# Casting transfers for the high parts of weights, and a shorter warm-up of TensorE

## The chip, the cores and the metric

The kernel runs on one core of a Trainium2 chip. The metric is the device time of one execution in microseconds (us). PE is TensorE, DVE is VectorE, ACT is ScalarE, POOL is GpSimd, SP is SyncE, which only issues transfers here.

## The reference

A causal convolution with seven taps per head, softmaxed over the taps, is followed by two blocks of two matrix products with an activation in between.

```python
w = softmax(weight, axis=-1)                            # 8 heads, 7 taps
x = causal_conv(x, w)                                   # 2 x 4096 tokens of 192 channels: 8192 x 192
h = x @ moe_w_in                                        # 192 -> 2048
g = np.where(h >= 1, h, np.where(h <= -1, 0.0, (h + 1) ** 2 / 4))
x = g @ moe_w_out                                       # 2048 -> 192
h = x @ moe2_w_in
out = (h / (1.0 + np.exp(-1.702 * h))) @ moe2_w_out
```

The weights arrive as 64-bit floats, everything else as 32-bit floats.

## The kernel before

The 8192 tokens are cut into 16 blocks of 512. Channels lie on partitions: part a is channels 0 to 127, part b the other 64, two blocks of part b in one tile. A phase is one block through one of the two matrix blocks `n` (1 or 2); it has 16 units, one for each 128 hidden channels (index `f`). A unit is five products into a bank `h` (`gemm1`), the activation (`act_a`), a split of its result into `ghi` and `glo` (`act_b`), and five products into the accumulators `acc` (`gemm2`), four units later (`LAG`).

To keep fp32 precision with the fast fp32r format, each operand is split into a high part, the value rounded to fp32r, and a low part, the rest: `split` casts on ACT (L74) and subtracts on DVE (L75). Products of high and low parts are added up in the same bank.

A weight tile is 128 x 448 words for each `n` and `f`, 32 tiles in all. It is loaded once as raw 64-bit words (`raw`) and turned into fp32 by integer operations, then split. `weight_ops` gives four pieces: `begin` (L118 on ACT, L119 on DVE), `join` (L123 on DVE), `high_part` (L129, a cast on ACT, or on DVE for the six tiles of `BY_DVE`) and `low_part` (L133 and L134 on DVE). The result lies in `wt` for the whole run. The first four tiles (`f < CH`, `n == 1`) are converted in the opening. The others follow a plan by steps: a step is one unit on TensorE, and `convert_at` puts the four pieces of a tile on four steps in a row, behind the unit's own work. Every engine takes its instructions in the order in which they are written (the schedule is manual).

In the opening TensorE first runs a warm-up, products of the identity with itself. The convolution of the first blocks is split between DVE (part a of block 0, tile `cva`), and TensorE with ACT and POOL: for each tap, a diagonal matrix (`diag`, the identity times the tap, L170) is multiplied with the shifted tile `xt`, seven products into `cb_ps` for part b of blocks 0 and 1 (diagonals made by ACT) and seven into `ca_ps` for part a of block 1 (diagonals made by POOL). `put_a` and `put_b` split the results into `xah`, `xal` and `xb`. These products are plain fp32, which the profile lists as two rows each. The opening's order on DVE and ACT is written out by hand:

```python
order = a0[0:5] + ws[0][0:1]
order += [lambda: nc.scalar.activation(table, ident[:, 0:1], AF.Gelu_apprx_sigmoid)]
order += ws[0][1:3] + a0[5:7] + ws[0][3:4] + ws[1][0:1] + [lambda: put_a(0, ca)]
order += ws[1][1:2] + [lambda: put_b(0, cb_ps)] + ws[1][2:] + ws[2]
```

Here `a0` are the seven convolution steps of block 0 on DVE, `ws[f]` the four pieces of weight tile `f`. The first unit's products need `wt`, `xah`, `xal` and, for the fourth and fifth, `xb`.

Of the kernel before, what the change touches and what calls it, by code (L numbers as in the profile page):

```python
# [8 lines left out]
F32 = mybir.dt.float32  # L9
F32R = mybir.dt.float32r  # L10
U32 = mybir.dt.uint32
# [4 lines left out]
P = 128  # L16
T = 512
# [3 lines left out]
def kernel(  # L21
# [21 lines left out]
    nc = tc.nc  # L43
    NBLK, D, _ = out.shape
    K = taps_in.shape[2]
    NF, _, WC = w1.shape
# [4 lines left out]
    LAG = 4  # L51
    CH = 4
    WHOLE = 2 * NF
    BY_DVE = {(1, f) for f in range(CH, NF, 3)} | {(2, 0), (2, 3)}

    const = ctx.enter_context(tc.tile_pool(name="const", bufs=1))
    wpool = ctx.enter_context(tc.tile_pool(name="wpool", bufs=1))
    stage = ctx.enter_context(tc.tile_pool(name="stage", bufs=2))
# [2 lines left out]
    xs_p = ctx.enter_context(tc.tile_pool(name="xs", bufs=4))  # L61
    a_p = ctx.enter_context(tc.tile_pool(name="a", bufs=3))
    g_p = ctx.enter_context(tc.tile_pool(name="g", bufs=LAG))
    o_p = ctx.enter_context(tc.tile_pool(name="o", bufs=2))
    ps = ctx.enter_context(tc.tile_pool(name="ps", bufs=1, space=bass.MemoryType.PSUM))

    def bank(n, name):
        return ps.tile([P, T], F32, tag=f"bank{n}", name=name)

    def f32(ap):  # L70
        return ap.bitcast(F32)
# [6 lines left out]
    taps = const.tile([P, 2, K], F32, name="taps")  # L78
    ident = const.tile([P, P], F32, name="ident")
    const.tile([P, 56], F32, name="pad")  # L80

    def softmax_taps():
        mx = const.tile([P, 2], F32, name="mx")
        sm = const.tile([P, 2], F32, name="sm")
        nc.vector.tensor_reduce(mx, taps, axis=AX.X, op=ALU.max)
        nc.vector.tensor_sub(taps, taps, mx.unsqueeze(2).to_broadcast([P, 2, K]))
        nc.scalar.activation(taps, taps, AF.Exp)
        nc.vector.tensor_reduce(sm, taps, axis=AX.X, op=ALU.add)
        nc.vector.tensor_scalar_add(sm, sm, 1e-9)
        nc.vector.reciprocal(sm, sm)  # L90
        nc.vector.tensor_mul(taps, taps, sm.unsqueeze(2).to_broadcast([P, 2, K]))


    words = {1: w1, 2: w2}
    wt = {n: wpool.tile([P, NF, 2 * WC], F32R, name=f"wt{n}") for n in (1, 2)}

    def weight_load(n, f):
# [4 lines left out]
    def weight_ops(n, f, s):  # L102

        low, high = s[:, :, 0], s[:, :, 1]  # L110
        w = wt[n][:, f, :]
        m = WC - DB
        st = {}

        def begin():
            a = stage.tile([P, WC], F32, tag="wa", name="wa")
            d = stage.tile([P, WC], U32, tag="wd", name="wd", bufs=3)
            nc.scalar.activation(a, f32(high), AF.Prelu, scale=2.0**-112, alpha=-(2.0**32))  # L118
            nc.vector.tensor_single_scalar(d, low, 29, op=ALU.logical_shift_right)  # L119
            st["a"], st["d"] = a, d  # L120

        def join():
            nc.vector.scalar_tensor_tensor(  # L123
                st["d"], st["a"].bitcast(U32), 3, st["d"], op0=ALU.logical_shift_left, op1=ALU.bitwise_or
            )

        def high_part():
            cast = nc.vector.tensor_copy if (n, f) in BY_DVE else nc.scalar.copy
            cast(w[:, 0:WC], f32(st["d"]))  # L129

        def low_part():
            d = f32(st["d"])
            nc.vector.tensor_sub(w[:, WC + DB : 2 * WC], d[:, 0:m], f32(w[:, 0:m]))  # L133
            nc.vector.tensor_sub(w[:, WC : WC + DB], d[:, m:WC], f32(w[:, m:WC]))  # L134

        return [begin, join, high_part, low_part]


    x1, x2 = {}, {}

    def new_xs():
        return [xs_p.tile([P, T], F32R, tag=t, name=t) for t in ("xah", "xal", "xb", "xc")]
# [16 lines left out]
    def warm_up():  # L159

        w = bank(7, "warm")
        wide = ident.unsqueeze(1).to_broadcast([P, T // P, P])
        for _ in range(4):
            nc.tensor.matmul(w.rearrange("p (k c) -> p k c", c=P), ident, wide, start=True, stop=True)  # L164

    def conv_on_pe(part, t, c, ident, eng_mul):

        d = o_p.tile([P, K, P], F32, tag="o", name="diag")
        for k in range(K):
            eng_mul(d[:, k], ident, taps[:, part, k : k + 1])  # L170

        def tap(k):
            return lambda: nc.tensor.matmul(c, d[:, k], t[:, k : k + T], start=k == 0, stop=k == K - 1)  # L173

        return [tap(k) for k in range(K)]

    def put_a(i, c):
        split(c, *x1[i][:2])
# [236 lines left out]
    plan, xt, raw = {}, {}, {}  # L415

    def at(step, op):
        plan.setdefault(max(step, 0), []).append(op)

    def fetch_w(n, f):  # L420
        raw[n, f] = weight_load(n, f)

    def weights_at(n, f):
        ops = []

        def piece():
            if (n, f) in raw:
                ops.extend(weight_ops(n, f, raw.pop((n, f))))
            ops.pop(0)()

        return [piece] * 4

    def fetch_x(*which):
        for part, i in which:
            xt[part, i] = x_load(part, i)
# [11 lines left out]
    with tc.manual_schedule():  # L447
        nc.sync.dma_start(taps, taps_in)
        fetch_x((0, 0), (1, 0))
        fetch_w(1, 0)  # L450
        fetch_w(1, 1)
        fetch_x((0, 1))
        fetch_w(1, 2)

        make_identity(nc, ident)
        warm_up()
        softmax_taps()

        table = const.tile([P, 1], F32, name="table")
        for i in range(B):  # L460
            x1[i] = new_xs()
        ca = cv_p.tile([P, T], F32, tag="cva", name="cva")
        cb_ps, ca_ps = bank(3, "cb_ps"), bank(2, "ca_ps")
        a0 = conv_taps(0, xt[0, 0], ca)
        b_ops = conv_on_pe(1, xt[1, 0], cb_ps, ident, nc.scalar.mul)
        a1 = conv_on_pe(0, xt[0, 1], ca_ps, ident, nc.gpsimd.tensor_scalar_mul)
        for op in b_ops + a1[:1]:
            op()

        ws = [weight_ops(1, f, raw.pop((1, f))) for f in range(CH - 1)]  # L470
# [4 lines that stand above are left out]
        for op in order:  # L475
            op()
        fetch_w(1, 3)
        for k, op in enumerate(weights_at(1, 3)):
            at(k // 2, op)
        for k, op in enumerate(a1[1:]):  # L480
            at(1 + k // 3, op)
        at(1, lambda: put_b(1, cb_ps))
        at(2, lambda: put_a(1, ca_ps))

        def convert_at(n, f, steps):
            at(steps[0] - 3, lambda: fetch_w(n, f))
            for step, op in zip(steps, weights_at(n, f)):
                at(step, op)

        for f in range(CH, NF):  # L490
            s = f - 2 if f < 2 * CH else 2 * CH - 1 + 5 * (f - 2 * CH) // 3
            convert_at(1, f, range(s, s + 4))
        for f in range(NF):
            s = (22, 23, 25, 26, 28, 29, 30, 31)[f] if f < NF // 2 else 36 + (3 * f - 3 * NF // 2) // 2
            convert_at(2, f, range(s, s + 4))
        for j in range(1, NBLK // B):
            conv_at(j)

        def beside(step):
            for op in plan.get(step, []):  # L500
                op()

        def finish_if_last(u, step):
            if 0 <= u < len(units) and units[u][1] == NF - 1:
                finish(units[u][0], step)


        for step in range(WHOLE):
            gemm1(step)
            if step >= LAG:  # L510
                gemm2(step - LAG)
            act_a(step)
            finish_if_last(step - LAG, step)
            if step >= 1:
                act_b(step - 1)
            if step == WHOLE - 1:
                act_b(step)
            beside(step)

        for u in range(WHOLE, len(units) + LAG + 4, 2):  # L520
            v = u - LAG
            if u == WHOLE:
                gemm1(u)
                gemm2(v)
                gemm1(u + 1)
                gemm2(v + 1)
            elif u < len(units):
                both(u, v)
            elif v < len(units):
                gemm2(v)  # L530
                gemm2(v + 1)
            if u < len(units):
                for op in (act_a, act_b):
                    op(u)
                    op(u + 1)
            for step in (u, u + 1):
                beside(step)
            finish_if_last(v + 1, u + 1)
# [55 lines left out]
```

## Time and profile before

| | |
|---|---|
| median of 3 runs | 1132.95 us (1132.06 to 1133.93) |
| profiled execution | 1132.19 us, its span 1130.4 us |
| PE busy | 1125.0 us, 9458 matmuls |
| weight loads (PEld) | 948.5 us |
| DVE busy | 716.0 us |
| ACT busy | 820.2 us |
| POOL busy | 6.5 us, 13 instructions |
| granted TensorE clock | 1.000 over the span |

The span runs from the first to the last instruction; the time of the execution holds about 1.8 us more. Times in the trace are counted from the start of the span. Ends of matmuls are modelled, so their starts say more than their lengths. The granted clock is listed as full for the whole span, the opening included.

### The profile page before, as it was taken

What the parts mean: (1) busy time and instruction counts of PE and PEld (TensorE: products, weight loads), DVE (VectorE), ACT (ScalarE), POOL (GpSimd) and SP (SyncE); (2) the same over time, 40 slices, a digit from 0 to 9 for tenths busy, and PEclk for the clock granted to TensorE, in tenths of its full rate; (3) what the DMA queues carried; (4) which work ended last, traced back from release to release, by engine and by line L of the source; (5) the groups of instructions that cost most, each with busy time, mean ns of one, the idle gap of its engine ahead of it and who ended that gap; (6) DMA issues with size and microseconds to landing.
All of it is one profiled execution on the core that took longest, in us unless ns stands there. A gap on an engine that the chain in (4) does not pass through costs nothing.

```text
span 1130.4 us, 23108 instructions
## 1 busy us (share of the span) xinstructions
PE 1125.0 (100%) x9458; PEld 948.5 (84%) x9458; DVE 716.0 (63%) x1158; ACT 820.2 (73%) x1462; POOL 6.5 (1%) x13
## 2 busy tenths in 40 slices
PE   9999999999999999999999999999999999999998
PEld 5888888888888888888888888888888888888887
DVE  7998867775647656475664756657566575655532
ACT  7998768867768677676876758677586776868654
POOL 2000000000000000000000000000000000000000
PEclk9999999999999999999999999999999999999999
DMA  5434111000010000100010000100001000000000
GB/s 160 135 112 159 34 34 44 11 20 15 11 39 15 20 15 14 36 15 20 15 41 22 1 20 15 48 15 1 20 15 48 15 1 20 15 20 15 11 15 15
DMA packets 16840, 36.68 MB, mean 32 GB/s; under 512 B 2528, under 2 KB 2784, under 8 KB 16736
## 3 DMA queue, kind: packets, MB, share of 16 engines
q1 hardware_dynamic: 16592, 35.09, 10.8%
q8 instruction: 74, 1.21, 0.5%
q14 instruction: 30, 0.25, 0.1%
q10 hardware_dynamic: 144, 0.13, 0.0%
HBM read 21.05 MB, written 6.29 MB: 24 GB/s over the span
## 4 chain that ended last, share of the span: by engine, by line
PE 100%; issue 0%; POOL 0%; ACT 0%; POOLq 0%
PE acc L366 48%; PE h L366 43%; PE acc L320 3%; PE h L255 3%; PE cb_ps L173 1%; PE ca_ps L173 1%; PE warm L164 0%; ACT o L410 0%; POOL ident masks.py:199 0%; POOL ident masks.py:197 0%; POOLq masks.py:199 0%; ACT o L408 0%; POOLq L580 0%
## 5 line engine op out<-in xcount | busy, mean ns | idle before, releaser
L366 PE MATMUL acc<-ghi,wt 64*128 64x512 f32 x2868 | 871.0, 386 | 0.0
L366 PE MATMUL h<-xah,wt 64*128 64x512 f32 x1912 | 738.2, 386 | 0.0
L366 PE MATMUL acc<-glo,wt 64*128 64x512 f32 x1912 | 706.7, 386 | 0.0
L366 PEld LDWEIGHTS acc<-ghi,wt 64*128 64x128 f32 x2868 | 490.9, 184 | 47.8
L75 DVE TENSOR_TENSOR glo<-a,ghi 128x512 fp32r<-128x512 f32 x512 | 341.6, 688 | 231.2 <-ACT ghi L74 220.9
L366 PEld LDWEIGHTS h<-xah,wt 64*128 64x128 f32 x1912 | 351.8, 184 | 32.4 <-issue 0.4
L366 PEld LDWEIGHTS acc<-glo,wt 64*128 64x128 f32 x1912 | 351.8, 184 | 32.2 <-DVE glo L75 0.2
L366 PE MATMUL h<-xal,wt 64*128 64x512 f32 x956 | 369.1, 386 | 0.0
L74 ACT CAST ghi<-a 128x512 fp32r<-128x512 f32 x512 | 301.5, 614 | 28.6 <-DVE a L279 28.4
L279 DVE SCALAR_TENSOR_TENSOR a<-h,a 128x512 f32<-128x512 f32 x256 | 176.8, 691 | 157.1 <-ACT a L278 156.7
L281 ACT ACTIVATE a<-h 128x512 f32<-128x512 f32 x256 | 150.3, 595 | 147.8 <-PE h L366 136.6
L366 PE MATMUL h<-xc,wt 64*128 64x512 f32 x717 | 238.7, 386 | 0.0
L366 PE MATMUL h<-xb,wt 64*128 64x512 f32 x717 | 238.7, 386 | 0.0
L277 ACT ACTIVATE a<-h 128x512 f32<-128x512 f32 x256 | 151.0, 590 | 53.9 <-PE h L366 53.3
L366 PEld LDWEIGHTS h<-xal,wt 64*128 64x128 f32 x956 | 175.9, 184 | 16.0
L278 ACT ACTIVATE a<-a 128x512 f32<-128x512 f32 x256 | 161.9, 632 | 8.2
L366 PEld LDWEIGHTS h<-xc,wt 64*128 64x128 f32 x717 | 131.9, 184 | 14.9
L366 PEld LDWEIGHTS h<-xb,wt 64*128 64x128 f32 x717 | 131.9, 184 | 9.1
L155 DVE SCALAR_TENSOR_TENSOR cva<-xt,taps,cva 128x512 f32<-128x512 f32 x90 | 67.4, 749 | 1.3
L155 DVE SCALAR_TENSOR_TENSOR cvb<-xt,taps,cvb 128x512 f32<-128x512 f32 x42 | 31.4, 747 | 0.5
L74 ACT CAST xb<-s 64x512 fp32r<-64x512 f32 x16 | 10.0, 623 | 29.2 <-DVE s L383 29.2
L320 PE MATMUL acc<-ghi,wt 128*128 128x512 f32 x102 | 29.0, 390 | 0.0
(62 smaller groups left out, 407.9 us busy)
## 6 DMA issues: line engine op xcount, KB each, us to landing
raw<-in_w_dram SPq DMA_DIRECT2D x32, 448.0 KB, 3.3
xc<-xb SPq DMA_DIRECT2D x46, 128.0 KB, 2.2
xt<-in_xa_dram SPq DMA_DIRECT2D x16, 259.0 KB, 2.9
out_dram<-o SPq DMA_DIRECT2D x15, 256.0 KB, 2.0
out_dram<-o SPq DMA_DIRECT2D x17, 128.0 KB, 2.3
xt<-in_xb_dram SPq DMA_DIRECT2D x8, 259.0 KB, 3.0
xb<-xc SPq DMA_DIRECT2D x14, 128.0 KB, 2.2
out_dram<-o ACTq DMA_DIRECT2D x1, 128.0 KB, 1.8
```

The costliest lines, as they stand in the source:

```text
L74: nc.scalar.copy(hi, src)
L75: nc.vector.tensor_sub(lo, src, f32(hi))
L155: return lambda: nc.vector.scalar_tensor_tensor(c, x, w, c, op0=ALU.mult, op1=ALU.add)
L173: return lambda: nc.tensor.matmul(c, d[:, k], t[:, k : k + T], start=k == 0, stop=k == K - 1)
L255: nc.tensor.matmul(h, w, r, start=j == 0, stop=j == len(prods) - 1)
L277: nc.scalar.activation(a, h, AF.Relu, bias=0.5, scale=0.5)
L278: nc.scalar.activation(a, a, AF.Square)
L279: nc.vector.scalar_tensor_tensor(a, h, 1.0, a, op0=ALU.max, op1=ALU.min)
L281: nc.scalar.activation(a, h, AF.Gelu_apprx_sigmoid)
L320: nc.tensor.matmul(acc, w, r, start=id(acc) in fresh, stop=last and ends[id(acc)] == k)
L366: mm = nc.tensor.matmul(banks[n], w, r, start=n in fresh, stop=ends.get(n) == k)
```

## The change

Three things change. The high parts of the 28 weight tiles that are not converted in the opening are written by transfers from POOL's queue, which read `wd` as fp32 and write `wt` as fp32r, instead of by a cast on ACT or DVE; `join` and `high_part` of these tiles are now on the same step, and the step after it is empty. The warm-up has two products instead of four, of a tile `ones` that DVE fills, and is written ahead of the identity. And buffers change: four `wd` instead of three, one output buffer instead of two, the diagonals of `ca_ps` in a set of `xs` buffers, a pad.

```diff
-    BY_DVE = {(1, f) for f in range(CH, NF, 3)} | {(2, 0), (2, 3)}
...
-    o_p = ctx.enter_context(tc.tile_pool(name="o", bufs=2))
+    o_p = ctx.enter_context(tc.tile_pool(name="o", bufs=1))
...
+    stage.tile([P, 64], F32, tag="pad", name="pad2", bufs=1)
...
-            d = stage.tile([P, WC], U32, tag="wd", name="wd", bufs=3)
+            d = stage.tile([P, WC], U32, tag="wd", name="wd", bufs=4)
...
         def high_part():
-            cast = nc.vector.tensor_copy if (n, f) in BY_DVE else nc.scalar.copy
-            cast(w[:, 0:WC], f32(st["d"]))
+            if n == 1 and f < CH:
+                nc.scalar.copy(w[:, 0:WC], f32(st["d"]))
+            else:
+                nc.gpsimd.dma_start(w[:, 0:WC], f32(st["d"]))
...
         w = bank(7, "warm")
-        wide = ident.unsqueeze(1).to_broadcast([P, T // P, P])
-        for _ in range(4):
-            nc.tensor.matmul(w.rearrange("p (k c) -> p k c", c=P), ident, wide, start=True, stop=True)
-
-    def conv_on_pe(part, t, c, ident, eng_mul):
-
-        d = o_p.tile([P, K, P], F32, tag="o", name="diag")
+        ones = const.tile([P, P], F32, name="ones")
+        nc.vector.memset(ones, 1.0)
+        wide = ones.unsqueeze(1).to_broadcast([P, T // P, P])
+        for _ in range(2):
+            nc.tensor.matmul(w.rearrange("p (k c) -> p k c", c=P), ones, wide, start=True, stop=True)
+
+    def conv_on_pe(part, t, c, ident, eng_mul, d):
+
         for k in range(K):
-            eng_mul(d[:, k], ident, taps[:, part, k : k + 1])
+            eng_mul(d[k], ident, taps[:, part, k : k + 1])
...
         def piece():
             if (n, f) in raw:
                 ops.extend(weight_ops(n, f, raw.pop((n, f))))
+                if n == 2 or f >= CH:
+                    begin, join, high, low = ops
+                    ops[1:3] = [lambda: (join(), high()), lambda: None]
             ops.pop(0)()
...
+        warm_up()
         make_identity(nc, ident)
-        warm_up()
...
-        b_ops = conv_on_pe(1, xt[1, 0], cb_ps, ident, nc.scalar.mul)
-        a1 = conv_on_pe(0, xt[0, 1], ca_ps, ident, nc.gpsimd.tensor_scalar_mul)
+        db = o_p.tile([P, K, P], F32, tag="o", name="diag")
+        da = [f32(t).rearrange("p (k c) -> p k c", c=P) for t in new_xs()]
+        b_ops = conv_on_pe(1, xt[1, 0], cb_ps, ident, nc.scalar.mul, [db[:, k] for k in range(K)])
+        da = [da[k // 4][:, k % 4] for k in range(K)]
+        a1 = conv_on_pe(0, xt[0, 1], ca_ps, ident, nc.gpsimd.tensor_scalar_mul, da)
```

DVE's order in the opening, before the change, from its first instruction of the kernel on (`mx`, `sm` and `taps` belong to the softmax of the taps):

```order
L85 TENSOR_REDUCE mx<-taps 128x2
L86 TENSOR_TENSOR taps<-taps,mx 128x14
L88 TENSOR_REDUCE sm<-taps 128x2
L89 TENSOR_SCALAR sm<-sm 128x2
L90 RECIPROCAL sm<-sm 128x2
```

The same place in the changed kernel:

```order
L165 MEMSET ones 128x128
L84 TENSOR_REDUCE mx<-taps 128x2
L85 TENSOR_TENSOR taps<-taps,mx 128x14
L87 TENSOR_REDUCE sm<-taps 128x2
L88 TENSOR_SCALAR sm<-sm 128x2
L89 RECIPROCAL sm<-sm 128x2
```

The memset stands first on DVE; what follows keeps its order, with other line numbers.

DVE's order from the join of weight tile 4 of matrix block 1 (`wd_260`) to its low part, before (`raw` and `wd` with other numbers are the next tiles'):

```order
L123 SCALAR_TENSOR_TENSOR wd_260<-wa_259,wd_260 128x448
L119 TENSOR_SCALAR wd_281<-raw_214 128x448
L279 SCALAR_TENSOR_TENSOR a_297<-h4_284,a_297 128x512
L75 TENSOR_TENSOR glo_302<-a_271,ghi_301 128x512
L129 CAST wt1_88<-wd_260 128x448
L123 SCALAR_TENSOR_TENSOR wd_281<-wa_280,wd_281 128x448
L119 TENSOR_SCALAR wd_308<-raw_238 128x448
L279 SCALAR_TENSOR_TENSOR a_324<-h5_313,a_324 128x512
L75 TENSOR_TENSOR glo_329<-a_297,ghi_328 128x512
L133 TENSOR_TENSOR wt1_88<-wd_260,wt1_88 128x384
```

The same place in the changed kernel, where the tile's `wd` is `wd_264`:

```order
L123 SCALAR_TENSOR_TENSOR wd_264<-wa_263,wd_264 128x448
L119 TENSOR_SCALAR wd_286<-raw_218 128x448
L282 SCALAR_TENSOR_TENSOR a_302<-h4_289,a_302 128x512
L74 TENSOR_TENSOR glo_307<-a_275,ghi_306 128x512
L123 SCALAR_TENSOR_TENSOR wd_286<-wa_285,wd_286 128x448
L119 TENSOR_SCALAR wd_313<-raw_242 128x448
L282 SCALAR_TENSOR_TENSOR a_329<-h5_318,a_329 128x512
L74 TENSOR_TENSOR glo_334<-a_302,ghi_333 128x512
L135 TENSOR_TENSOR wt1_89<-wd_264,wt1_89 128x384
```

The cast is gone from DVE's queue; the low part (now L135) stands at the same place and waits for the transfer, which POOL issues once the join is done. On POOL, whose instructions before the change ended with the diagonals, this is what stands from the identity on:

```order
masks.py:197 MEMSET ident 128x128
masks.py:199 ISA
masks.py:199 AFFINE_SELECT ident<-ident 128x128
L173 TENSOR_SCALAR xah<-ident,taps 128x128 x4
L173 TENSOR_SCALAR xal<-ident,taps 128x128 x3
L131 DMA wt_89<-wd 128x448 x12
L131 DMA wt_90<-wd 128x448 x16
```

The diagonals now lie in `xah` and `xal` buffers, and the 28 transfers, 12 for matrix block 1 and 16 for matrix block 2, are new.

## Rows read from the trace of the kernel before

**Rows 1.** The page's busy time: us, share of the span, instructions.

```profile
PE 1125.0 (100%) x9458; PEld 948.5 (84%) x9458; DVE 716.0 (63%) x1158; ACT 820.2 (73%) x1462; POOL 6.5 (1%) x13
```

**Rows 2.** The chain that ended last, in time: start, us, what.

```profile
13.83 2.40 PE h L255 x10
...
27.12 1.13 PE acc L320 x5
```

**Rows 3.** Timeline of the opening, TensorE: start, us, engine, line, what [idle <-releaser].

```profile
1.34 0.50 PEld L164 LDWEIGHTS warm<-ident 128*128 128x128 f32 x2 [1.34 <-POOL ident masks.py:199]
...
4.06 0.34 PEld L164 LDWEIGHTS warm<-ident 128*128 128x128 f32 x1 [0.52 <-issue]
...
4.92 0.34 PEld L164 LDWEIGHTS warm<-ident 128*128 128x128 f32 x1 [0.52 <-issue]
5.51 0.19 PEld L164 LDWEIGHTS warm<-ident 128*128 128x128 f32 x1 [0.26 <-issue]
...
6.80 6.17 PE L173 MATMUL cb_ps<-xt,diag 128*128 128x512 f32 x14
```

**Rows 4.** Timeline of the opening, POOL, SP, ACT; last, the landing of the 1.62 load.

```profile
0.71 0.20 POOL masks.py:197 MEMSET ident<- 128x128 f32 x1 [0.29 <-POOLq L580]
0.99 0.29 POOL masks.py:199 TENSOR_SCALAR_AFFINE_SELECT ident<-ident 128x128 f32<-128x128 f32 x1
...
1.62 0.43 SPq L147 DMA_DIRECT2D xt<-in_xb_dram  x1
...
4.06 2.16 ACT L170 ACTIVATE diag<-ident,taps 128x128 f32<-128x128 f32 x7 [0.91 <-DVE taps L91]
...
DMA to landing us min/median/max: 3.1/3.1/3.1
```

**Rows 5.** Timeline of the opening around the first `xb`.

```profile
11.65 0.62 DVE L123 SCALAR_TENSOR_TENSOR wd<-wa,wd 128x448 uint32<-128x448 uint32 x1
...
13.01 0.58 ACT L74 CAST xb<-cb_ps 64x512 fp32r<-64x512 f32 x1 [2.13 <-PE cb_ps L173]
...
13.62 0.69 DVE L75 TENSOR_TENSOR xb<-cb_ps,xb 64x512 fp32r<-64x512 f32 x1 [1.35 <-ACT xb L74]
...
14.37 0.73 PE L255 MATMUL h<-xb,wt 128*128 128x512 f32 x2
```

**Rows 6.** Groups by line: count, busy us, mean ns, idle before.

```profile
L129 ACT CAST wt<-wd 128x448 fp32r<-128x448 f32 x26 | 14.7, 566 | 7.9 <-DVE wd L123 7.7
...
L129 DVE CAST wt<-wd 128x448 fp32r<-128x448 f32 x6 | 2.3, 391 | 0.0
```

**Rows 7.** Windows: us; PE, PEld, DVE, ACT, POOL busy; clock, DMA share, GB/s.

```profile
5.00:10.00 5.00, 5.00 (x13) 2.34 (x12) 4.75 (x8) 4.31 (x10) 4.91 (x6) 1.00 0.92 330
...
30.00:35.00 5.00, 5.00 (x24) 4.14 (x23) 5.00 (x12) 4.94 (x10) 0.00 (x0) 1.00 0.59 184
```

**Rows 8.** Timeline: unit 8's `glo` on DVE and where TensorE takes it.

```profile
40.17 0.70 DVE L75 TENSOR_TENSOR glo<-a,ghi 128x512 fp32r<-128x512 f32 x1
...
43.51 0.61 PE L320 MATMUL acc<-glo,wt 128*128 128x512 f32 x2
```

**Rows 9.** Transfers: `xc<-xb` on the page; landings of all `raw` loads.

```profile
xc<-xb SPq DMA_DIRECT2D x46, 128.0 KB, 2.2
...
DMA to landing us min/median/max: 3.0/3.3/6.4
```

**Rows 10.** Timeline of DVE from 30 us: tiles 4, 6, 7 between units' work.

```profile
30.15 0.69 DVE L75 TENSOR_TENSOR glo<-a,ghi 128x512 fp32r<-128x512 f32 x1
30.75 0.55 DVE L133 TENSOR_TENSOR wt<-wd,wt 128x384 fp32r<-128x384 f32 x1
...
31.35 0.62 DVE L123 SCALAR_TENSOR_TENSOR wd<-wa,wd 128x448 uint32<-128x448 uint32 x1
31.89 0.39 DVE L119 TENSOR_SCALAR wd<-raw 128x448 uint32<-128x448 uint32 x1
32.19 0.69 DVE L279 SCALAR_TENSOR_TENSOR a<-h,a 128x512 f32<-128x512 f32 x1
```

More of the change, by code (lines that the diff above doesn't have):

```diff
@@ L161, in warm_up @@
         w = bank(7, "warm")
-        wide = ident.unsqueeze(1).to_broadcast([P, T // P, P])
-        for _ in range(4):
-            nc.tensor.matmul(w.rearrange("p (k c) -> p k c", c=P), ident, wide, start=True, stop=True)
-    def conv_on_pe(part, t, c, ident, eng_mul):
-        d = o_p.tile([P, K, P], F32, tag="o", name="diag")
+        ones = const.tile([P, P], F32, name="ones")
[4 more added lines that the diff above has]
+    def conv_on_pe(part, t, c, ident, eng_mul, d):
         for k in range(K):
-            eng_mul(d[:, k], ident, taps[:, part, k : k + 1])
+            eng_mul(d[k], ident, taps[:, part, k : k + 1])
         def tap(k):
-            return lambda: nc.tensor.matmul(c, d[:, k], t[:, k : k + T], start=k == 0, stop=k == K - 1)
+            return lambda: nc.tensor.matmul(c, d[k], t[:, k : k + T], start=k == 0, stop=k == K - 1)
         return [tap(k) for k in range(K)]
```

## Prediction

> **What bounds the kernel now.** I read the page's busy line first: TensorE is busy 1125.0 of 1130.4 us [rows 1]. Then the chain that ended last, in order of time. It is TensorE throughout: the first ten hidden products take 2.40 us from 13.83 on, and from 27.12 each unit is five products of the first GEMM and five of the second, 1.13 us each [rows 2]. No piece of it is a wait, so what ACT, DVE and the transfers do behind it costs nothing until TensorE runs dry. The end can move in two ways only: TensorE gets to its real work earlier, or something makes it wait.
>
> So the opening is to be read closely. The weight loads show the pace of the plain-fp32 products, two rows each. Two loads stand at 1.34 us; after them a row's load stands where the row before it starts. The fifth and sixth loads, at 4.06 and 4.92, are 0.86 us apart, the seventh follows at 5.51, and three rows later, at 6.80, `cb_ps` starts: 0.43 a row [rows 3]. These are the engine's two levels, 1.2 and 2.4 GHz. The rise lies in the row from 4.92 to 5.51, near 5.25 (1,024 columns in 0.59 us make 0.33 us at half pace and 0.26 at full). The warm-up's first four rows end at 4.92.
>
> **The warm-up.** *Start.* Now the first load follows the identity's last POOL step, 0.99 + 0.29 = 1.28 us, by 0.06 [rows 3, 4]. Afterwards it follows a memset of `ones` on DVE, which waits for nothing. POOL's first step of the kernel stands at 0.71 and is a memset of that size, 0.20 us [rows 4]. The trace has none on DVE: between nothing and 0.20 I take 0.20, so 0.91, a load at 0.95, and TensorE is 0.39 us earlier.
>
> *Length.* Two products leave four rows; at half pace they end 0.39 before 4.92, at 4.53. `cb_ps` then needs its first diagonal (ACT makes seven in 2.16 us from 4.06 on, the first near 4.4) and part b's `xt`, issued at 1.62 and landed 3.1 later, at 4.72 [rows 4]. So it starts near 4.78 instead of 6.80: 2.02 us are freed, and a gap of 0.25 is new. Its 14 rows take 14 × 0.43 = 6.02 us at full pace and end at 10.80; if the clock rises at 5.25 as now, at 11.03.
>
> *What ends last then.* TensorE next does one product of `ca_ps` and three of h0; the fourth needs `xb`. ACT starts casting its high part at 13.01, 0.2 us behind `cb_ps`; DVE starts the low part 0.61 later, at 13.62, and the product starts at 14.37 [rows 5], in a chain without a gap [rows 2]: today both are just in time. Afterwards `cb_ps` is early, but DVE takes its work in order, and in front of the low part stands the join of weight tile 1, at 11.65 [rows 5]. DVE is busy 4.75 of 5 us from 5 to 10 us [rows 7] with a chain that the change leaves alone (seven convolution steps, tile 0's conversion); the memset falls into its idle start. After a join DVE's next instruction starts 0.54 later (31.35 to 31.89) [rows 10], so here at 12.19. `xb`'s low part moves from 13.62 to 12.19, **1.43 us**, and the product from 14.37 to 12.94. Some 0.6 of the 2.02 us freed become a new wait for DVE at h0. This holds if `cb_ps` ends by 12.19 - 0.61 - 0.2 = 11.38.
>
> *Does it last?* Tile 1's low part and tile 2's conversion stand back to back behind `xb` on DVE and move with it; ACT's cast of tile 2 waits for that join, and ACT's later work follows it. The diagonals of `ca_ps` are the same seven POOL steps into other buffers. I count 1.43 us for the rest of the run.
>
> **The casts.** ACT loses 22 casts of 0.566 us and DVE six of 0.391 [rows 6], 12.5 and 2.3 us of work beside a TensorE that did not wait for it. Both are full there, 4.94 and 5.00 of 5 us from 30 to 35 [rows 7], yet early: DVE ends unit 8's `glo` at 40.87 and TensorE takes it at 43.51, 2.6 us later [rows 8], the smallest margin that I found. So the gain is nothing; only the margin grows.
>
> In return 28 transfers of 224 KB leave from POOL, whose queue is empty. No such transfer is in the trace. The nearest rows: 128 KB between buffers of this kind land in 2.2 us, 448 KB from DRAM in 3.0 to 6.4, median 3.3 [rows 9]; they cast nothing and leave from SP. I take 3.5 (nearer to the first, with some preparation on POOL), bounds 2.2 and 6.4.
>
> Behind the low part that waits for the landing, DVE holds every later `glo`. What is the deadline? Tiles 8 to 15 are converted in pairs of 3.33 steps, 3.33 × 2.27 = 7.56 us of TensorE. The first tile's low part stands two steps after its join, the second's join lies in between. So DVE needs per pair the landing L and, outside it, a join (0.54), two low parts (0.60 each), a begin (0.30) and 1.33 steps of its unit work (2 × 0.60 each, 1.6) [rows 10]: L + 3.6 us. Up to L = 3.9 it keeps pace; above, each pair sets it back by L - 3.9. Some seven pairs (the first 12 tiles and the start of the next 16) share the margin of 2.6, so TensorE waits from L = 3.9 + 2.6/7 = 4.3 on, 7 us for each us more. At 3.5 the transfers cost nothing; DVE stops at some low parts, and nobody waits for it.
>
> A row that speaks against: DVE's shift at 31.89 takes 0.39 us where its two-input join of the same width takes 0.62 [rows 10]; it runs in a faster mode, once per tile. If POOL cannot prepare a transfer meanwhile, that is 0.39 once or twice: 3.9 to 4.3, still at no price. The Trainium skill, SBUF — State Buffer, "Who interferes with whom", says that DVE in a two-port mode locks GpSimd out of the port that it writes descriptors through; the section "SBUF: two separate sides" tells of a POOL transfer of 620 ns that took 3100 beside a DVE copy. With those 2.5 us on top of 2.2 a landing would be an estimated 4.7, and the sum 3 us longer, about 1134.2. No run here shows it.
>
> The other edits cost nothing: outputs (one buffer now) are a phase apart, and the fourth set of `xs`, lent to the diagonals, is wanted only when the first phase ends.
>
> **Sum.** The profiled execution took 1132.19 us (span 1130.4, 1.8 around it): 1132.19 - 1.43 = 1130.76. The runs' median, 1132.95, is 0.76 above; with the same shift, 1131.52. The runs spread from 1132.06 to 1133.93, and the opening offers a reason: each us by which the clock rises later costs half a us on TensorE's path. If that makes the 0.76, the median run rises 1.5 us later. Afterwards, 0.39 earlier, its rise would be at 5.25 - 0.39 + 1.5 = 6.36; `cb_ps` still ends by 11.38 with a rise at 5.94, and the rest costs half of 0.42: 1130.97. Between 1130.97 and 1131.52 I take **1131.2**.
>
> **Rivals.**
> *A cold opening (most of the gain lost).* With half the warm-up and a gap behind it, the clock may rise only later. For: four rows fewer, a new gap. Against: TensorE is about as full as before, `cb_ps` only takes the warm-up's place. It decides from a rise at 5.94 on; at 8.3 it costs (8.3 - 5.94)/2 = 1.2: 1132.4. All of `cb_ps` at half pace, 6 us more less the cover of 0.6, would be 1136; I give that next to nothing.
>
> *Late transfers (slower).* DVE stops at the low parts, `glo` comes late, TensorE stops. It decides from a landing of 4.3 us on; with 4.85 the gain and the 0.2% are gone (3.9 us lost, 1135.2), with the bound of 6.4 it is 7 × 2.5 - 2.6 = 14.9 us, 1146. For: the 6.4, DVE's faster mode, a cast on the way. Against: 6.4 stands in the opening, where the DMA engines are busy 0.92; from 30 to 35 us they are at 0.59 [rows 7].
>
> *A larger gain.* If late rises are usual before and covered afterwards, the difference passes 2.27 us: 1130.5. It needs no new mechanism, only the spread.
>
> **Chances.** A measurement of this kernel tells 0.2%, 2.27 us, from no change. The forecast and the larger gain together 0.67, of which 0.31 beyond 2.27 us; cold opening 0.12 and slightly late transfers (landing 4.3 to 4.85) 0.06, both within; late transfers 0.15, slower. Faster 0.31, same 0.54, slower 0.15. The range: 1129.8 (DVE's memset at its lower bound, all of the spread covered) to 1134.0 (transfers near 4.7); it leaves out the late transfers and the coldest openings. The forecast's own is 1130.3 to 1132.0.
>
> **What would show it.** Right: `cb_ps` starts near 4.8 and ends near 11; `xb`'s first low part stands near 12.2, with TensorE idle some 0.6 us before it; the later pieces come 1.4 us earlier throughout; ACT holds four casts of weights, DVE none; transfers from POOL land in 3 to 4.3 us, and where DVE waits for one, TensorE does not. Wrong: rows of `cb_ps` 0.86 apart beyond 6 us; TensorE idle before `glo` with DVE waiting for a landing; or an opening as forecast and a time around the span that grew.

## The result, and the profile after

| | before | after |
|---|---|---|
| median of 6 runs each | 1132.74 us (1132.06 to 1133.93) | 1142.01 us (1141.27 to 1143.07) |
| profiled execution, span | 1132.19, 1130.4 us | 1141.27, 1139.5 us |

The changed kernel is slower: the ratio is 1.0084, 95% interval [1.0074, 1.0094]. The forecast of 1131.2 us is missed, with its sign and its range.

The page of the changed kernel: busy time (it answers to [rows 1]), the low parts of the weight tiles with what ended DVE's idle time before them, and the new transfers with their median landing.

```profile
PE 1127.6 (99%) x9454; PEld 931.2 (82%) x9454; DVE 714.0 (63%) x1153; ACT 812.0 (71%) x1440; POOL 21.4 (2%) x41
...
L135 DVE TENSOR_TENSOR wt<-wd,wt 128x384 fp32r<-128x384 f32 x32 | 17.7, 554 | 22.4 <-DMA wt<-wd 21.6
...
wt<-wd POOLq DMA_DIRECT2D x28, 224.0 KB, 4.1
```

TensorE's busy share has hardly moved and says nothing of 9 us. The waits do (what waited for what: us in total, times, longest):

```profile
DVE wt L135 <- DMA wt<-wd: 21.6, 13, 4.8
...
PE h L258 <- DVE xb L74: 4.0, 2, 3.7
```

**The opening** went as forecast. Its timeline (start, us, engine, line, what; in brackets idle time and releaser) answers to [rows 3 to 5]:

```profile
0.82 0.17 DVE L165 MEMSET ones<- 128x128 f32 x1 [0.82 <-PEq L589]
...
1.04 0.50 PEld L168 LDWEIGHTS warm<-ones 128*128 128x128 f32 x2 [1.04 <-DVE ones L165]
...
4.91 0.67 PE L176 MATMUL cb_ps<-xt,diag 128*128 128x512 f32 x1 [0.44 <-DMA xt<-in_xb_dram]
...
10.99 1.02 PE L176 MATMUL ca_ps<-xt,xah 128*128 128x512 f32 x2
...
11.58 0.62 DVE L123 SCALAR_TENSOR_TENSOR wd<-wa,wd 128x448 uint32<-128x448 uint32 x1
...
12.23 0.68 DVE L74 TENSOR_TENSOR xb<-cb_ps,xb 64x512 fp32r<-64x512 f32 x1
...
12.97 0.50 PE L258 MATMUL h<-xb,wt 128*128 128x512 f32 x1 [0.27 <-DVE xb L74]
```

TensorE starts 0.30 us earlier, `cb_ps` ends by 10.99, and h0's fourth product stands at 12.97 instead of 14.37: 1.40 us gained. At the first weight tile that comes through a transfer TensorE is still 1.36 us ahead (31.27 against 32.63, the unit's first product).

**Where it is lost.** Three stretches, by the same place in the program. First, the first transfer, of weight tile 4. DVE's, POOL's and SP's rows from 25 us, and the low part that waits:

```profile
24.85 0.62 DVE L123 SCALAR_TENSOR_TENSOR wd<-wa,wd 128x448 uint32<-128x448 uint32 x1
25.39 0.39 DVE L119 TENSOR_SCALAR wd<-raw 128x448 uint32<-128x448 uint32 x1
25.78 0.71 POOL L131 DMA_DIRECT2D wt<-wd  x1 [15.94 <-DVE wd L119]
25.85 2.50 SPq L99 DMA_DIRECT2D raw<-in_w_dram  x2
...
31.19 0.56 DVE L135 TENSOR_TENSOR wt<-wd,wt 128x384 fp32r<-128x384 f32 x1 [1.91 <-DMA wt<-wd]
```

The join's row ends at 25.47 (24.85 + 0.62), POOL issues at 25.78 and the transfer lands 5.4 us later. 0.07 us behind the issue SP issues the next raw load of 448 KB, since the shift begun at 25.39 has just freed its buffer. The unit that uses this tile starts at 31.27, so its second product waits for the low part. Before the change the low part of the same tile, begun at 30.75 [rows 10], ended at 31.22 + 0.22 = 31.44, and its unit started at 32.63. Second piece of the low part and first product, kernel before:

```profile
31.22 0.22 DVE L134 TENSOR_TENSOR wt<-wd,wt 128x64 fp32r<-128x64 f32 x1
...
32.63 0.61 PE L255 MATMUL h<-xah,wt 128*128 128x512 f32 x2
```

That margin is 1.2 us, and for tile 7 it is 0.6 (38.82 to 39.43), not 2.6. TensorE is 1.36 us ahead at tile 4's unit and 0.48 late at tile 7's (39.91 against 39.43), so 1.84 us are lost.

Second, the step from matrix block 1 to 2. POOL, SP, DVE and TensorE, changed kernel:

```profile
83.01 0.53 POOL L131 DMA_DIRECT2D wt<-wd  x1 [5.39 <-DVE wd L119]
...
83.08 0.33 SPq L99 DMA_DIRECT2D raw<-in_w_dram  x1
...
88.41 0.56 DVE L135 TENSOR_TENSOR wt<-wd,wt 128x384 fp32r<-128x384 f32 x1 [2.46 <-DMA wt<-wd]
...
91.28 0.69 DVE L74 TENSOR_TENSOR xb<-s,xb 64x512 fp32r<-64x512 f32 x1
...
92.02 0.74 PE L258 MATMUL h<-xb,wt 128*128 128x512 f32 x2 [3.72 <-DVE xb L74]
...
92.92 1.48 PE L323 MATMUL acc<-ghi,wt 128*128 128x512 f32 x3
94.19 1.05 PE L323 MATMUL acc<-glo,wt 128*128 128x512 f32 x2
```

Behind the low part that waits for its landing stands `xb`, the first input of matrix block 2. Before, it was written at 85.19 and read at 87.48, with 85.19 + 0.69 = 85.88 a margin of 1.6 us. Its write and its first use, kernel before:

```profile
85.19 0.69 DVE L75 TENSOR_TENSOR xb<-s,xb 64x512 fp32r<-64x512 f32 x1
...
87.48 0.62 PE L255 MATMUL h<-xb,wt 128*128 128x512 f32 x2
```

Now it starts at 91.28 and TensorE stands still for 3.72 us. And then it runs at half pace: three products from 92.92 to 94.19, 0.42 us each, where they are 0.23 apart elsewhere. Two windows (busy times, then the granted clock, DMA share, GB/s) show it:

```profile
80.00:100.00 20.00, 16.28 (x73) 12.69 (x73) 15.90 (x33) 14.66 (x27) 2.11 (x4) 0.91 0.62 165
...
93.00:96.00 3.00, 3.00 (x9) 2.33 (x8) 3.00 (x8) 2.97 (x6) 0.53 (x1) 0.50 0.67 113
```

At the same product TensorE is 0.65 us late at 87.68 (before 87.03) and 6.28 late at 96.71 (before 90.43): 5.6 us lost, 3.7 as the wait and 1.9 at half pace.

Third, some 2.7 us between 100 and 146 us, where DVE again stands at a low part and TensorE needs `glo` behind it:

```profile
119.11 0.56 DVE L135 TENSOR_TENSOR wt<-wd,wt 128x384 fp32r<-128x384 f32 x1 [4.79 <-DMA wt<-wd]
...
120.76 0.50 PE L369 MATMUL acc<-glo,wt 64*128 64x512 f32 x1 [0.29 <-DVE glo L74]
...
131.07 0.49 PE L369 MATMUL acc<-glo,wt 64*128 64x512 f32 x1 [1.38 <-DVE glo L74]
```

The transfer that the first of these rows waits for was issued at 112.10 and took 7.0 us; three `xt` loads and a raw load had been issued from 110.50 to 112.02. At the end the span is 9.1 us longer.

**Two kinds of landings.** Of the 28 transfers twelve are issued within 0.1 us of a raw load and land in 4.2 to 7.0 us; two more, 0.9 us behind a load and 2.1 us behind the last of a run of five loads, take 5.0 and 5.9. Around the issue of the other fourteen there is no load from DRAM within 1.2 us; thirteen of them take 2.2 to 3.0 us, one 3.9.

The packets show what a slow transfer waits for. Tile 8 of matrix block 1 is issued at 40.74, a raw load 0.07 us later. First what moved from 40.74 to 43.64, then from there to 45.10 (queue, packets, MB, share of 16 engines; `q1` is the loads' queue, `q0` POOL's, which holds 28 x 144 packets and is not on the page of the kernel before):

```profile
q1 hardware_dynamic: 114, 0.40, 56.3%
...
q0 software_dynamic: 284, 0.46, 100.0%
q1 hardware_dynamic: 30, 0.05, 9.6%
```

For 2.9 us not one packet of the transfer moves, while the load moves 0.40 of its 0.46 MB; then this transfer and the next go through. With nothing beside it (103.75) a transfer's first packet comes 1.1 us after the issue. A load that is issued 1.27 us behind a transfer, as at tiles 10 and 13 of matrix block 1, hardly holds it up: they land in 2.2 and 2.6 us.

### The profile page after: what moved, and what is told of

Read it like the earlier page. It is cut to its first block, busy times and chain, and to the rows that moved or that the text cites. A ratio compares the mean times of both kernels' runs of the same rounds, so it can differ in the third digit from the quotient of the medians.

```text
span 1139.5 us, 23149 instructions
## 1 busy us (share of the span) xinstructions
PE 1127.6 (99%) x9454; PEld 931.2 (82%) x9454; DVE 714.0 (63%) x1153; ACT 812.0 (71%) x1440; POOL 21.4 (2%) x41
## 4 chain that ended last, share of the span: by engine, by line
PE 91%; DMA 4%; DVE 3%; issue 1%; ACT 1%; POOL 0%; DVEq 0%; POOLq 0%
PE acc L369 47%; PE h L369 42%; DMA wt<-wd 3%; PE acc L323 1%; PE h L258 1%; DVE wd L123 1%; DVE glo L74 0%; DVE wd L119 0%; DVE cva L157 0%; DVE wt L135 0%; DVE a L282 0%; DVE wt L136 0%; ACT a L281 0%; ACT a L280 0%; DMA taps<-in_taps_dram 0%
## 5 line engine op out<-in xcount | busy, mean ns | idle before, releaser
L369 PEld LDWEIGHTS acc<-ghi,wt 64*128 64x128 f32 x2868 | 486.0, 184 | 53.0
L135 DVE TENSOR_TENSOR wt<-wd,wt 128x384 fp32r<-128x384 f32 x32 | 17.7, 554 | 22.4 <-DMA wt<-wd 21.6
```

Of the source, the lines that this page charges most:

```text
L369: mm = nc.tensor.matmul(banks[n], w, r, start=n in fresh, stop=ends.get(n) == k)
```

## The experiments

There are two theories. *Shared engines*: a transfer is slow while a 448 KB load is in flight, since both use the same DMA engines. *Port lock*: DVE's shift L119, 0.39 us in its faster mode, holds POOL up, as weighed in the prediction. Each kernel is the changed one with the edit shown, and its ratio is to the kernel before, with a 95% interval; the median of before was 1132.52 us beside the first four and 1132.39 beside the others.

**1. The warm-up alone**

```diff
+    BY_DVE = {(1, f) for f in range(CH, NF, 3)} | {(2, 0), (2, 3)}
...
-            if n == 1 and f < CH:
-                nc.scalar.copy(w[:, 0:WC], f32(st["d"]))
-            else:
-                nc.gpsimd.dma_start(w[:, 0:WC], f32(st["d"]))
+            cast = nc.vector.tensor_copy if (n, f) in BY_DVE else nc.scalar.copy
+            cast(w[:, 0:WC], f32(st["d"]))
...
-                if n == 2 or f >= CH:
-                    begin, join, high, low = ops
-                    ops[1:3] = [lambda: (join(), high()), lambda: None]
```

> New warm-up and buffers, casts on ACT and DVE as before the change. Both theories of the slow landings agree here: only the opening's gain is left. The first fourth product of h0 starts near 12.97 us as in the changed kernel, the pieces of 1.13 us stand 1.4 us ahead of the kernel before, no wait of TensorE after 13 us. Time 1132.7 - 1.4 to 2.0 = 1130.7 to 1131.3, ratio 0.9982 to 0.9988. If the other edits (one output buffer, borrowed xs buffers, pads) cost anything, it shows here as a time above 1131.5.

Measured: 1131.06 us (11 runs, 1130.83 to 1131.33), ratio 0.9987 [0.9978, 0.9995]. By the medians the opening is worth 1132.52 - 1131.06 = 1.46 us; TensorE waits for nothing after the first `xb`, and the buffer edits cost nothing that shows. The profiled run falls short of the forecast: the fourth product of h0 stands at 13.39, not 12.97, since DVE's join in front of `xb` starts at 12.01 and not at 11.58, and the later products are 0.96 us ahead of the kernel before, not 1.4. This version beats both kernels.

**2. The transfers alone**

```diff
-        ones = const.tile([P, P], F32, name="ones")
-        nc.vector.memset(ones, 1.0)
-        wide = ones.unsqueeze(1).to_broadcast([P, T // P, P])
-        for _ in range(2):
-            nc.tensor.matmul(w.rearrange("p (k c) -> p k c", c=P), ones, wide, start=True, stop=True)
+        wide = ident.unsqueeze(1).to_broadcast([P, T // P, P])
+        for _ in range(4):
+            nc.tensor.matmul(w.rearrange("p (k c) -> p k c", c=P), ident, wide, start=True, stop=True)
...
+        make_identity(nc, ident)
         warm_up()
-        make_identity(nc, ident)
```

> Old warm-up (four products of the identity), casts by transfers from POOL. If the two parts simply add: 1142.0 + 1.4 to 2.0 = 1143.4 to 1144.0. If the loss depends on how the transfers happen to meet the loads of raw weights, it may differ by 2 us either way: 1141 to 1146. Landings 2.2 to 7 us as in the changed kernel.

Measured: 1141.73 us, ratio 1.0084 [1.0070, 1.0098]; landings 2.2 to 7.7 us; TensorE waits 3.7 us for `xb` and 2.1 for `glo`. The transfers alone make the loss. The opening's gain does not add up beside them: this kernel is 0.3 us ahead of the changed one, not 1.46 behind. In the profiles two thirds of it are spent on waiting: TensorE is 1.54 us behind the changed kernel here at tile 4's unit (32.81 against 31.27) and 0.47 behind at tile 7's (40.38 against 39.91), since an earlier TensorE waits longer for the low parts. Later the distance grows to 1.33 us (98.04 against 96.71), because the stretch at half pace is longer in this profile: its window from 80 to 100 us has a granted clock of 0.83 where the changed kernel's has 0.91. Over all runs the granted clock averages 0.998 in both kernels, so half pace does not tell the medians apart; why they keep nothing of the gain is open.

**3. The shift as a two-input operation of the same result**

```diff
+    sevens = const.tile([P, 1], U32, name="sevens")
...
-            nc.vector.tensor_single_scalar(d, low, 29, op=ALU.logical_shift_right)
+            nc.vector.scalar_tensor_tensor(
+                d, low, 29, sevens.to_broadcast([P, WC]), op0=ALU.logical_shift_right, op1=ALU.bitwise_and
+            )
...
+        nc.vector.memset(sevens, 7)
```

> The changed kernel, with DVE's shift of each weight tile written as a two-input operation (0.62 us instead of 0.39, same result), so that DVE never runs in its faster mode beside POOL's preparation of a transfer. Theory 'port lock' (POOL is held by that mode): landings fall to 2.2 to 3 us throughout, DVE waits under 3 us in all for transfers, time near 1131.5. Theory 'shared engines' (a transfer is slow while a 448 KB load from DRAM is in flight on the same DMA engines): landings stay at 2.2 to 7, median near 4, and DVE has 28 x 0.23 us more work, time 1142 to 1146.

Measured: 1140.47 us, ratio 1.0073 [1.0059, 1.0087], landings 2.2 to 7.3, median 3.4: faster than the 1142 to 1146 expected with shared engines, and far from the 1131.5 of the port lock. Its rows at tile 4 (DVE, POOL):

```profile
25.85 0.62 DVE L126 SCALAR_TENSOR_TENSOR wd<-wa,wd 128x448 uint32<-128x448 uint32 x1
26.39 0.62 DVE L120 SCALAR_TENSOR_TENSOR wd<-raw,sevens 128x448 uint32<-128x448 uint32 x1
...
26.79 0.71 POOL L134 DMA_DIRECT2D wt<-wd  x1 [16.43 <-DVE wd L126]
```

The join's row ends at 26.47 and POOL issues 0.32 us later, in the middle of the shift; with the fast shift it was 0.31 after the join, and POOL's own work is 0.71 us in both. So the shift's mode moves neither. The slow landings stay at the same tiles; eleven of the twelve are 0.3 to 1.4 us shorter, and the longest is 7.3 instead of 7.0. The slower shift also lets the raw load go 0.2 us later, which fits the first theory, but no run here shows that this is the reason. The changed kernel itself has a transfer with the fast shift in front of it and no load issued beside it, and it lands in 2.2 us (DVE, POOL; tile 6 of matrix block 2):

```profile
100.73 0.38 DVE L119 TENSOR_SCALAR wd<-raw 128x448 uint32<-128x448 uint32 x1
...
101.10 0.53 POOL L131 DMA_DIRECT2D wt<-wd  x1 [4.42 <-DVE wd L119]
```

The port lock is not the cause of the slow landings. What a lock would do to POOL's own work is not tested: the fast shift's row ends where POOL's begins (25.39 + 0.39 = 25.78).

**4. No raw loads after the first four tiles** (later tiles are made from the words of earlier ones, so the result is that of other weights)

```diff
+    kept = []
...
-        raw[n, f] = weight_load(n, f)
+        if n == 1 and f < CH:
+            kept.append(weight_load(n, f))
+            raw[n, f] = kept[-1]
+        else:
+            raw[n, f] = kept[1 + f % 3]
```

> The changed kernel without the loads of raw weights after the first four tiles: the later tiles are converted from the buffers that already lie in SBUF, so all conversion work and all 28 transfers stay and only the load traffic is left out (the result is then that of other weights). Theory 'shared engines': landings 2.2 to 3 us throughout, DVE waits for transfers under 2 us in all, TensorE does not wait after 13 us, time 1130.5 to 1131.5. Theory 'port lock': landings as in the changed kernel, median near 4, up to 7, time near 1142.

Measured: 1131.36 us, ratio 0.9991 [0.9982, 1.0001]. The page's row of the transfers, and DVE's waits for them:

```profile
wt<-wd POOLq DMA_DIRECT2D x28, 224.0 KB, 2.2
```

```profile
DVE wt L135 <- DMA wt<-wd: 3.7, 4, 1.4
```

All 28 transfers are still there, and the loss is gone: TensorE waits for nothing after 13 us. DVE's waits and seven landings of 3.0 to 4.2 us are more than expected, and cost nothing. But transfers that are never in the way are no faster than the casts that they replace: 1131.36 against 1131.06.

**5. Half of each later raw load** (the other half of the tile keeps earlier words; the result is again that of other weights)

```diff
...
+            s = kept[1 + (NF * (n - 1) + f - 1) % 3]
+            half = WC // 2
+            nc.sync.dma_start(s[:, 0:half].rearrange("p c t -> p (c t)"), words[n][f].bitcast(U32)[:, 0 : 2 * half])
+            raw[n, f] = s
```

The lines in front of these are those of experiment 4.

> The changed kernel, but from weight tile 4 on only half of the columns of a raw tile is loaded (224 KB instead of 448 KB); the other half keeps an earlier tile's words, so the result is that of other weights. Issue times and DVE's fast-mode shift stay. Shared engines (a transfer is slow as long as a raw load is in flight): the transfers issued beside a load should land about halfway between 2.2 and the 4.2 to 7.0 us of the changed kernel, 3 to 4.6 us, and the time should come out far nearer to the kernel without later loads (1131.4 us) than to the changed one (1142.0): 1131.4 to 1135. Port lock (the shift holds POOL): landings as in the changed kernel, median 4.1, and 1140 to 1143 us.

Measured: 1132.30 us, ratio 0.9999 [0.9989, 1.0008]; landings 2.2 to 5.9, median 3.2. Landings of the same tiles under three doses, us:

| matrix block, tile | full load | half | none |
|---|---|---|---|
| 1, 4 | 5.4 | 5.0 | 4.0 |
| 1, 5 | 5.9 | 4.1 | 2.6 |
| 1, 6 | 4.4 | 3.6 | 2.2 |
| 1, 7 (no load issued beside it) | 2.7 | 2.3 | 2.2 |
| 1, 8 | 4.2 | 3.6 | 2.2 |
| 2, 2 | 5.4 | 3.8 | 2.1 |
| 2, 8 (`xt` loads too) | 7.0 | 5.9 | 4.0 |

The landing follows the size of the load beside it. Without raw loads tile 4's 4.0 stays, as do five more of 3.0 to 4.2 us beside which there is no load either. What these six have, and tile 8 of matrix block 2, is a packet from one of the queues that the page lists as `instruction`, in flight while their own packets move. For the longest, tile 12 of matrix block 2 (experiment 4, 117.02 to 118.90):

```profile
q0 software_dynamic: 135, 0.22, 36.7%
q8 instruction: 1, 0.02, 6.0%
```

Of the other 21 transfers of that kernel one has such a packet at its very end and the others none in that time; they land in 2.1 to 2.6 us. No run leaves these packets out, so that they cause the delay is likely but not shown.

**6. and 7. Transfers for one matrix block, casts for the other**

```diff
...
-                if n == 2 or f >= CH:
+                if n == 1 and f >= CH:
```

and in the seventh kernel `if n == 2`, with the same condition around the transfer itself and the casts of before behind its `else`.

> The changed kernel, but only the 12 weight tiles of matrix block 1 that the plan converts go through transfers; the 16 of matrix block 2 are cast on ACT and DVE as before. By the account of the trace (lost: 1.7 us in units 8 to 11 on tiles 4 to 7, some 0.2 more by 83 us, the rest only with block 2): 1.9 us above the kernel with the warm-up alone (1131.06), 1133.0, range 1132.3 to 1133.7. If instead each of the 28 transfers sets DVE back by a like amount, 12/28 of the 10.95 us: 1135.7.

> The changed kernel, but only the 16 weight tiles of matrix block 2 go through transfers; the 12 of matrix block 1 are cast on ACT and DVE as before. By the account of the trace (about 8.3 to 9 us lost from 83 to 146 us): 1139.4 to 1140.1 us, with the first long wait of TensorE before a fourth product of a block 2 unit near 88 us, for xb. If each of the 28 transfers costs alike, 16/28 of 10.95 us: 1137.3.

Measured: block 1 alone 1135.14 us, ratio 1.0024 [1.0014, 1.0033], block 2 alone 1137.16 us (4 runs, 1134.92 to 1137.68), ratio 1.0039 [1.0024, 1.0054]. Above the warm-up alone that is 4.1 and 6.1 us, near the equal share of each transfer (4.7 and 6.3) and not near my account by time (1.9 and 8.3 to 9.0). The account gave the 3.72 us wait to block 2, because it stands there. In the sixth kernel's profile TensorE is 0.86 us late at tile 7's unit (40.29 against 39.43), and the span ends 2.4 late: it waits for `xb` at the start of block 2, although every tile of block 2 is cast:

```profile
88.87 0.74 PE L260 MATMUL h<-xb,wt 128*128 128x512 f32 x2 [0.36 <-DVE xb L75]
```

With block 1 cast, the same tile's transfer is issued earlier, and `xb` is in time (POOL and DVE of the seventh kernel):

```profile
78.35 0.53 POOL L130 DMA_DIRECT2D wt<-wd  x1 [4.96 <-DVE wd L124]
```

```profile
83.07 0.56 DVE L137 TENSOR_TENSOR wt<-wd,wt 128x384 fp32r<-128x384 f32 x1 [1.78 <-DMA wt<-wd]
...
85.94 0.68 DVE L75 TENSOR_TENSOR xb<-s,xb 64x512 fp32r<-64x512 f32 x1
```

The transfer goes at 78.35 instead of 83.01. TensorE is only 1.5 us earlier there (81.69 against 83.15), so 3.2 us of the 4.7 are DVE's own lateness, piled up over block 1's twelve transfers and called in at the next tight place. The profiled run of the seventh kernel took 1134.92 us, only 3.9 above the warm-up alone, so the nearness of 6.1 to the equal share says little. The other three took 1.9 to 2.8 us more, with a granted clock of 0.998 over the span where the profiled one has 1.000. That is worth an estimated 0.002 x 1136 = 2.3 us, so a stretch at half pace is likely there; the wait in front of it is not seen.

**8. Transfers without a cast** (these high parts are not rounded, and the low parts are zero)

```diff
-                nc.gpsimd.dma_start(w[:, 0:WC], f32(st["d"]))
+                nc.gpsimd.dma_start(f32(w[:, 0:WC]), f32(st["d"]))
```

> The changed kernel, but the 28 transfers copy the words as they are, without a cast to fp32r; the high parts of these tiles are not rounded, and their low parts are zero. If the cast on the way makes a transfer long, landings alone fall below 2.2 us, those beside a load below 4.2, and the time falls below 1140. Shared engines: landings as in the changed kernel (2.2 alone, 4.2 to 7.0 beside a load), 1140.5 to 1143 us.

Measured: 1139.78 us, ratio 1.0068 [1.0053, 1.0083]; landings 2.1 to 6.2, median 4.0. By their letter the signs that I had set for the cast came out, each by a hair: 2.1 alone, 4.1 at the least beside a load, a time below 1140 and below the 1140.5 to 1143 of shared engines. Their size speaks against it: without a cast the shortest landing falls by 0.04 us (2.15 to 2.11) and tile 8's by 0.10 (4.22 to 4.12). So the cast is not what makes them late. The medians differ from the changed kernel's by 2.2 us, the profiled runs by 1.2 (1140.05 against 1141.27). In the profiles that arises after 107 us, where the longest landing is 6.2 instead of 7.0; whether it is the cast or the moment of the issue is open.

## Why the prediction was wrong

**The opening: right.** 1.43 us forecast, 1.40 in the changed kernel's trace and 1.46 between the medians of experiment 1. That they agree so closely is partly luck: experiment 1's own profile shows 0.96. DVE's memset took 0.17, not 0.20, TensorE started at 1.04 instead of 0.95, and both fell into the cover that was counted. DVE's join in front of `xb` became the limit, as reckoned. The cold opening did not happen: `cb_ps`'s rows come 0.43 us apart from 5.41 on.

**The casts cost nothing to leave out, and gain nothing: right.** Experiment 4 shows it: with landings of 2.2 us the kernel stands where it stands with the casts.

**"I take 3.5 (nearer to the first, with some preparation on POOL), bounds 2.2 and 6.4": the step that failed.** The two bounds lie near the two kinds of landing, 2.2 alone and 4.2 to 7.0 beside a load; the median was 4.1. One value between them describes neither. I put the 6.4 aside because "6.4 stands in the opening", and that was read wrongly. Landings of the raw loads of the kernel before, first those issued up to 16 us, then the later ones; last, the window with the 6.4, of a load issued at 106.15 behind three `xt` loads and another raw load:

```profile
DMA to landing us min/median/max: 3.1/3.9/6.2
...
DMA to landing us min/median/max: 3.0/3.3/6.4
...
105.00:112.00 7.00, 7.00 (x66) 5.78 (x64) 4.92 (x11) 5.71 (x12) 0.00 (x0) 1.00 0.96 350
```

So the 6.4 stood in mid-run, at the place where the changed kernel's transfer took 7.0. The other half of the reason was that "from 30 to 35 us they are at 0.59". A mean share over 5 us does not tell what stands at one moment: the join that releases the transfer is followed at once by the shift that releases the next raw load, so the two collide by order of the program, at 12 of the 28 tiles. The order shown ahead of the prediction has L123 and L119 in neighbouring rows; that was to be read. The Trainium skill, DMA: Bandwidth & Descriptors, "Issuing engines are not separate DMA queues", says that transfers started by the scalar, sync or gpsimd engine run on the same 16 engines and interleave. Experiments 4 and 5 agree that an empty queue on POOL is no free path, with 2.2, 3.6 and 4.4 us for tile 6 without, with half and with a full load. Of interleaving the trace shows little: at tile 8 the transfer's packets come behind most of the load's.

**"2.6 us later, the smallest margin that I found": the second step.** It was the margin of `glo` alone. The low part itself has 1.2 down to 0.6 us at tiles 4 to 7, which come one a step and not two in 3.33 steps, and `xb` of matrix block 2 has 1.6. With "from L = 4.3 on" the median of 4.1 would have cost nothing; the transfers cost 1142.01 - 1131.06 = 10.95 us. What decides is the single landing against the next deadline behind it, plus the lateness that DVE still carries; that lateness adds up over tiles, as the pair reckoning had it (experiments 6 and 7).

**A term that was missing: TensorE's pace after a wait.** After 3.72 us of standing still the clock was at its lower level (granted clock 0.50 from 93 to 96 us), and 1.9 us were lost. The window from 80 to 100 us tells it in the experiments too: 0.83 to 0.91 in those in which TensorE waits 2.9 to 3.7 us for `xb` there (2, 3 and 8), 1.00 in those in which it waits at most 0.5 (5, 6 and 7).

**The rival.** Late transfers had 0.15 and a price of 1135.2 at 4.85 us and 1146 at 6.4. The mechanism and its place, DVE held at low parts with `xb` and `glo` behind, are what came, at 1142.0; the chance was too small. The reason given against 6.4 was wrong, and nothing tied the transfer to the load.

**The port lock** was one of the reasons held against the change. Experiment 3 shows no such hold-up: POOL issues 0.3 us after the join's end under either shift. The estimate of 4.7 us lies among the slow landings, but not for the reason given.

## What to carry to other kernels

When work moves from an engine to a transfer, look in the program's order for what else is issued in the same moment: a transfer issued together with a load waited here until most of the load had moved, and a mean DMA share does not show it. List every consumer behind the waiting instruction with its own margin, and take the smallest; lateness on an engine is called in later, at a place that did not cause it. Where the replaced work costs the limiting engine nothing, even a perfect transfer gains nothing: here the warm-up alone, 1131.06 us, is the version to keep.

## What the runs showed of the hardware

A 224 KB transfer from POOL between SBUF tiles lands in 2.1 to 2.2 us when nothing else is in flight, cast or no cast, and in 4.2 to 7.0 in the changed kernel when it is issued with a load of 448 KB. Its first packet then came 2.9 us after the issue (tile 8), alone 1.1. POOL issues it 0.3 us after the end of the operation it waits for, and is busy 0.53 us with it, 0.71 the first time. After a wait of 3.72 us in mid-run TensorE's products came 0.42 us apart instead of 0.23, at a granted clock of 0.50.
